# One core: other places for the weight decoding, the pair sums and half of the softmax sums in the first pass of a fused attention and two-layer MLP kernel

## The chip, the core and the metric

The kernel runs on one core of a Trainium2 chip. The engines are TensorE (PE, with its weight loads PEld), VectorE (DVE), ScalarE (ACT), GpSimd (POOL) and SyncE (SP), which issues nearly all DMAs. Each engine works through its own queue in order; an instruction whose inputs or buffer aren't ready holds everything behind it on that engine. The metric is the device time of one launch in microseconds (us), as the median of several runs.

## What is computed

```python
def _attn_ref(q, k, v):                      # 8 batches, 8 heads, 576 tokens, 64 dims
    k_p = k.reshape(B, H, Sp, pool, D).mean(axis=3)      # pooled by 8: 72 keys
    v_p = v.reshape(B, H, Sp, pool, D).mean(axis=3)
    scores = scale * np.matmul(q, k_p.transpose(0, 1, 3, 2))
    attn = softmax(scores)
    return np.matmul(attn, v_p)
x = attention, as 4608 tokens x 512
h = x @ w_in; g = h * np.cos(h); x = g @ w_out                    # 512 -> 2048 -> 512
h = x @ w2_in; solu = h * softmax(h); x = layernorm(solu) * g_ln; out = x @ w2_out   # 512 -> 1024 -> 512
```

The weights come as float64 and are turned into float32 on the core by integer work on their two words. Every product is made of three float32r matmuls of high and low parts.

## The kernel before

The tokens are cut into nine blocks of 512. Pass one makes `h = x @ w_in` for all blocks and stores `g`; pass two multiplies by `w_out`; the last part does the second layer. The change is in pass one.

Pass one is written by hand as a list of places. A block has eight units, a unit eight places: 64 places (`BL`) a block. At each place PE gets three `h` matmuls (`h_mm`, line 652) and then whatever other work was put there with `put(place, function)`; every engine's queue gets its instructions in that order. A place fixes only the order, not a time: an engine runs ahead until something it needs is late. In the numbering here, block 1 starts with the first score matmul at 117.78 us of the trace; block 0 lies before it.

While a block's `h` matmuls run, its places also carry:

- the chain of `h * cos(h)` for the units before: ACT lines 663 and 669, DVE lines 666 and 671;
- the attention of the next token block (`Attn.plan`). Scores of four head pairs at places 0 to 21, their maxima and subtractions on DVE (lines 422, 423) three places behind, exponentials on ACT at 13 and 25. Then, for each half of the heads, `norm`: row sums and reciprocals on DVE (lines 499 to 503, at 16 and 28), and three places later the scaling on POOL (lines 509, 514). Then for each half two transpositions of the scaled weights (`e_tr`, line 550, tile eTp) with one of the left-over part between them (`e_tr_left`, eLp), at 27, 30, 33 and 42, 45, 48, and the products with v (`av`, line 577, tile xo) at 36, 39 and 51, 54. Each of these writes a PSUM tile of the pool `ps_a`, which has two buffers; ACT copies the tile out (eT, eL, x), DVE subtracts that copy from it (lines 555, 533, 580), and only then is the buffer free for the second transposition, score or product behind it;
- the pooling of the next k and v on POOL (lines 231, 259, 273) and the preparation of v (`prep_v`: POOL, ACT and, as its third step, four DVE instructions, lines 367 to 372);
- the weights of the later layers, 24 chunks of 128x512 (`Chunk.plan`). Each is loaded into one of two `raw` buffers, opened by two ACT instructions (`s1`, lines 114 and 115), unpacked by three DVE instructions (`bits`, lines 119, 123, 127) and joined on POOL (`join`, line 139). Chunks 0 to 7 are `w2_in`; each four are followed by `weight_sums` (four DVE subtractions, line 804) and `weight_parts`. Chunks 8 to 23 are `w_out`; each two are followed by `w_sums`, called pair sums here (four DVE instructions, line 877).

Before, a chunk stands every 16 places, at places 0, 16, 32 and 48 of a block; the `w_out` chunks begin 32 places later than that row would have it, so block 3 has chunks at 32 and 48 only, and blocks 4 to 6 at all four.

Of the kernel before, what the change touches and what calls it, by code (L numbers as in the profile page):

```python
# [35 lines left out]
def fused_kernel(ctx, tc, qT_d, kT_d, vN_d, vM_d, vL_d, w_in, w_out, w2_in, w2_out, g_ln, out):  # L36
# [4 lines left out]
    nc = tc.nc  # L41
# [7 lines left out]
    KD = DM // P  # L49
# [51 lines left out]
    class Chunk:  # L101
# [43 lines left out]
        def s3(self):  # L145
            self.done(self)

        def plan(self, put, o, raw, ahead=10):
            put(o - ahead, self.load, raw)
            put(o, self.s1)  # L150
            put(o + 4, self.bits)
            put(o + 7, self.join)
            if self.g is not None:
                put(o + 10, lambda: nc.vector.tensor_scalar(
                    out=self.f, in0=self.f, scalar1=self.g, scalar2=None, op0=ALU.mult))
            self.done(put, o, self)
# [5 lines left out]
    def two(put, o, hi, lo, f):  # L162
        put(o, lambda: nc.scalar.activation(out=hi(), in_=f(), func=AF.Copy))
        put(o + 2, lambda: nc.gpsimd.tensor_tensor(
            out=lo(), in0=f(), in1=hi().bitcast(F32), op=ALU.subtract))
# [214 lines left out]
    class Attn:  # L380
# [206 lines left out]
        def plan(self, put):  # L587
            new = [b for _, _, b, s in self.sg if s == 0 and b > 1]
            nxt = [b for _, _, b, s in at[self.j + 1].sg if s == 0] if self.j < NB - 1 else []

            def staged(pos, make, *a):

                fns = []
                put(pos[0], lambda: (fns.extend(make(*a)), fns[0]()))
                for i, q in enumerate(pos[1:]):
                    put(q, lambda i=i: fns[i + 1]())

            if self.j == 1:
                for i in range(2):
                    put(2 + 4 * i, add, 1, 1, KV[i])  # L600
                    put(17 + 8 * i, pool_vn, 1, i)
                    staged((20 + 8 * i, 22 + 8 * i, 24 + 8 * i), prep_vn, 1, i)
            for p in range(NPAIR):
                for u in range(2):
                    o = 6 * p + 3 * u
                    staged((o, o + 3), self.scores, p, u)
                put((13, 13, 25, 25)[p], self.exp, p)
            for b in new:
                staged((14, 17, 21), prep_v, b)
            for hf in range(2):  # L610
                o = (16, 28)[hf]
                staged((o, o + 3), self.norm, 2 * hf, 2 * hf + 1)
                o = 27 + 15 * hf
                for i, (fn, n) in enumerate((
                        (self.e_tr, 2 * hf), (self.e_tr_left, hf), (self.e_tr, 2 * hf + 1),
                        (self.av, 2 * hf), (self.av, 2 * hf + 1))):
                    d = (2, 4) if fn == self.av else (1, 3)
                    staged((o + 3 * i, o + 3 * i + d[0], o + 3 * i + d[1]), fn, n)
            for p in range(NPAIR):
                if self.j > 1:  # L620
                    put(-10 + 6 * p, self.load_q, p)
            for b in new:
                for i in range(6):
                    put(-10 + 2 * i, kv_load, b, i // 3, KV[2 + i % 3])
                    put(2 * i + i // 3, add, b, i // 3, KV[2 + i % 3])
            for b in nxt:
                for i in range(4):
                    put(32 + 3 * i, kv_load, b, i // 2, KV[i % 2])
                    put(42 + 3 * i, add, b, i // 2, KV[i % 2])

    NQ = NF // 2
# [174 lines left out]
    def weight_parts(put, o, i):  # L806

        k, n = divmod(i, 4)
        t = {}

        def tile():
            if not t:
                t[0] = wo.tile([P, 2, BLK], F32R, "tw")
            return t[0]

        two(put, o, lambda: tile()[:, 0], lambda: tile()[:, 1],
            lambda: whole[((k, 0), (k, 1), (KH + k, 1), (KH + k, 0))[n]])
        put(o + 6, put_away, wd_tw[i], tile)
# [46 lines left out]
    def w_whole(f):  # L865
        w_f[f] = ap1.tile([P, BLK], F32, tag=("qT", "e")[f % 2], name="wf", bufs=2)
        return w_f[f]
# [13 lines left out]
    def w_chunk(f):  # L881
        q = f // 2

        def done(put, o, c):
            if q < 6:
                put(o + 9, lambda: nc.sync.dma_start(out=wf[2 * q][:, 1 - f % 2], in_=w_f[f]))
            if f % 2:
                put(o + 10, w_sums, q)
                if q < 6:
                    put(o + 13, lambda: nc.sync.dma_start(  # L890
                        out=wf[2 * q + 1].rearrange("p a (b n) -> p (a b) n", n=NH), in_=w_s[q]))
                else:
                    w_parts(put, o + 13, q)
        return Chunk(w_out_w[f], done, whole=lambda: w_whole(f))

    wq = {(q, k): dram.tile([P, 2 if k < 3 else 1, 2, NH], F32R, tag=f"wq{k}", name=f"wq{q}{k}", bufs=2)
# [2 lines left out]
    def w_parts(put, o, q):  # L899
        t = {}  # L900

        def part(k, w):
            if k not in t:
                t[k] = wo.tile([P, 2 if k < 3 else 1, 2, NH], F32R, "wp")
            return t[k][:, :, w]

        for i, (k, c, src) in enumerate((
                (0, slice(0, 2), lambda: w_s[q][:, 0:2]), (1, slice(0, 2), lambda: w_s[q][:, 2:4]),
                (2, slice(0, 1), lambda: w_f[2 * q + 1][:, 0:NH]),
                (2, slice(1, 2), lambda: w_f[2 * q][:, 0:NH]),  # L910
                (3, slice(0, 1), lambda: w_f[2 * q][:, NH:BLK]))):
            def end(w, k=k, c=c):
                x = part(k, w)[:, c]
                return x if k < 2 else x.rearrange("p a n -> p (a n)")
            two(put, o + 2 * i, lambda end=end: end(0), lambda end=end: end(1), src)
        for k in range(4):
            put(o + (4, 6, 10, 12)[k], lambda k=k: nc.sync.dma_start(
                out=wq[q, k].bitcast(F32), in_=t[k].bitcast(F32)))
# [244 lines left out]
    def new_raws(tag):  # L1163
        return [xp.tile([P, BLK, 2], I32, tag=tag, name=f"raw{i}") for i in range(4)]
# [26 lines left out]
    with tc.manual_schedule():  # L1191
        raws = new_raws("x0")
# [91 lines left out]
        SL = 2 * KD  # L1284
        BL = NQ * SL
        work = [[] for _ in range(BL * NB + SL * NQ)]

        def put_at(j):
            def put(pos, fn, *a):
                work[BL * (j - 1) + pos].append(lambda: fn(*a))  # L1290
            return put
# [5 lines left out]
        raws = [ap1.tile([P, BLK, 2], I32, tag=t, name="raw") for t in ("em", "eT")]  # L1297
# [3 lines left out]
        chunks += [w_chunk(f) for f in range(NF)]  # L1301
        put = put_at(2)
        for i, c in enumerate(chunks):
            c.plan(put, 2 * SL * (i + 2 * (i // NQ > 0)), raws[i % 2])
        for k in range(KH):
            o = 2 * SL * KD * (k + 1) + 3
            put(o, weight_sums, k)
            for i in range(KD):
                weight_parts(put, o + 4 + 6 * i, KD * k + i)
        put = put_at(NB)  # L1310
        for q, o in enumerate((4, 11, 18, 25, 32, 42)):
            put(o - 9, w_load, q)
# [41 lines left out]
        raws = [wo.tile([P, BLK, 2], I32, "raw", 12 + i) for i in range(2)]  # L1354
# [6 lines left out]
        for m in range(len(units)):  # L1361
            j, q = units[m]
# [100 lines left out]
        a, b, c = NTL - 4, NTL - 3, NTL - 2  # L1463
# [72 lines left out]
```

## Time and profile before

| | |
|---|---|
| median of 3 runs | 1343.4 us (1339.92 to 1344.93) |
| the profiled execution | 1341.87 us |
| its span, first to last instruction | 1340.0 us |
| PE busy | 1305.3 us, 97% |
| DVE busy | 1053.8 us, 79% |
| ACT busy | 697.1 us, 52% |
| POOL busy | 500.7 us, 37% |
| mean granted PE clock | 0.992 of full speed |

Pass one with its attention lies between about 75 and 566 us, pass two and the second layer behind it. A busy PE is a PE with a matmul under way; where it waits, the trace names the instruction that released it.

### The profile page before, as it was taken

To read this page: it belongs to the slowest core of one execution; us is meant where nothing else is said; L and a number is where in the kernel's file an instruction comes from. 1 tells how busy PE (TensorE), PEld (TensorE's weight loads), DVE (VectorE), ACT (ScalarE), POOL (GpSimd) and SP (SyncE) were. 2 spreads that over 40 slices of the span, in tenths; PEclk is the share of its full clock that TensorE was granted. 3 is DMA by queue.
4 is the path that set the end of the run, shared out by engine and by line. 5 is a ranking of instruction groups with operands and counts; after the bars stand their busy time and mean duration, and the time that the engine had idled before them with its cause. 6 is when DMAs were issued, how large, how long until landed. Compare 5 with 4: busy or idle time off the path is not lost. (4 is left out here: it accounts for less than half of the span.)

```text
span 1340.0 us, 20553 instructions
## 1 busy us (share of the span) xinstructions
PE 1305.3 (97%) x7574; PEld 1139.2 (85%) x7574; DVE 1053.8 (79%) x1675; ACT 697.1 (52%) x987; POOL 500.7 (37%) x668
## 2 busy tenths in 40 slices
PE   6889999999999999999999999999999999999998
PEld 5768777887887888899999999999878888888887
DVE  7798887978879785779889899885777767676753
ACT  4576765756566576634444444443544444444432
POOL 3497676765544243501100001101443434343410
PEclk8899999999999999999999999999999999999999
DMA  8425666674655446665555455568411111111101
GB/s 287 169 83 189 217 240 217 235 258 161 236 202 203 149 183 237 221 244 147 156 155 168 141 173 170 153 212 323 146 40 48 40 55 40 56 40 56 40 25 40
DMA packets 82133, 206.09 MB, mean 154 GB/s; under 512 B 7920, under 2 KB 26352, under 8 KB 82032
## 3 DMA queue, kind: packets, MB, share of 16 engines
q1 hardware_dynamic: 81888, 204.77, 44.9%
q8 instruction: 60, 0.98, 0.3%
q14 instruction: 41, 0.34, 0.1%
q10 hardware_dynamic: 144, 0.00, 0.0%
HBM read 125.57 MB, written 79.17 MB: 153 GB/s over the span
## 5 line engine op out<-in xcount | busy, mean ns | idle before, releaser
L652 PE MATMUL h<-x,w 128*128 128x512 f32 x1728 | 434.8, 400 | 0.3 <-DVE t L671 0.3
L652 PEld LDWEIGHTS h<-x,w 128*128 128x128 f32 x1728 | 316.2, 189 | 64.3 <-issue 2.8
L744 PE MATMUL y<-g,wy 128*128 128x256 f32 x3024 | 363.8, 283 | 1.7 <-DVE g L718 1.1
L744 PEld LDWEIGHTS y<-g,wy 128*128 128x128 f32 x3024 | 363.2, 192 | 2.3 <-DVE g L718 1.5
L716 ACT CAST g<-gs 128x1024 fp32r<-128x1024 f32 x72 | 75.7, 1051 | 173.2 <-PE y L744 82.3
L139 POOL TENSOR_TENSOR dec<-dec,raw 128x512 int32<-128x512 int32 x24 | 33.7, 1403 | 240.2 <-DVE dec L127 227.9
L718 DVE TENSOR_TENSOR g<-gs,g 128x1024 fp32r<-128x1024 f32 x72 | 90.3, 1254 | 34.6 <-ACT g L716 32.3
L669 ACT ACTIVATE t<-t,cst 128x1024 f32<-128x1024 f32 x72 | 83.0, 1152 | 57.5 <-DVE t L666 57.4
L671 DVE TENSOR_TENSOR t<-t,h 128x1024 f32<-128x1024 f32 x72 | 87.3, 1213 | 18.0 <-ACT t L669 18.0
L974 POOL TENSOR_TENSOR yl<-yr,yh 128x1024 fp32r<-128x1024 f32 x18 | 44.0, 2446 | 153.8 <-ACT yh L969 153.8
L663 ACT ACTIVATE t<-h 128x1024 int32<-128x1024 f32 x72 | 73.3, 1019 | 42.9 <-PE h L652 42.9
L666 DVE SCALAR_TENSOR_TENSOR t<-t,h 128x1024 f32<-128x1024 int32 x72 | 87.2, 1211 | 1.2 <-ACT t L663 1.2
L231 POOL TENSOR_TENSOR kvraw<-kvraw 128x256 f32<-128x256 f32 (+1 forms) x124 | 80.4, 648 | 12.0 <-DMA kvraw<-in_vL 2.3
L1105 POOL TENSOR_TENSOR sc<-sc,cst 128x1 f32<-128x1 f32 x36 | 20.4, 566 | 140.5 <-DVE sc L1094 113.1
L1140 ACT COPY o<-o 128x512 f32<-128x512 f32 x36 | 21.2, 588 | 96.7 <-PE o L1158 96.7
L698 DVE TENSOR_TENSOR gs<-gr,gs 128x256 f32<-128x256 f32 x136 | 65.9, 484 | 4.7
L718 DVE TENSOR_TENSOR g<-gr,g 128x768 fp32r<-128x768 f32 x68 | 69.1, 1016 | 0.0
L1156 PE MATMUL o<-w,lh 128*128 128x512 f32 x176 | 69.0, 392 | 0.0
L1158 PE MATMUL o<-w,ll 128*128 128x512 f32 x176 | 68.5, 389 | 0.0
L1157 PE MATMUL o<-w,lh 128*128 128x512 f32 x176 | 68.5, 389 | 0.0
L139 POOL TENSOR_TENSOR wf<-dec,raw 128x512 int32<-128x512 int32 x24 | 31.4, 1308 | 67.9 <-DVE dec L127 35.7
L716 ACT CAST g<-gr 128x768 fp32r<-128x768 f32 x68 | 56.6, 832 | 0.0
(191 smaller groups left out, 2571.6 us busy)
## 6 DMA issues: line engine op xcount, KB each, us to landing
gd<-t SPq DMA_DIRECT2D x72, 512.0 KB, 3.0
gr<-gd SPq DMA_DIRECT2D x68, 512.0 KB, 4.0
raw<-in_w_in SPq DMA_DIRECT2D x24, 512.0 KB, 4.8
raw<-in_w_out SPq DMA_DIRECT2D x24, 512.0 KB, 5.1
kvraw<-in_kT SPq DMA_DIRECT2D x32, 288.0 KB, 4.4
qT<-in_qT SPq DMA_DIRECT2D x36, 256.0 KB, 4.7
yd<-yo SPq DMA_DIRECT2D x36, 256.0 KB, 4.6
yr<-yd SPq DMA_DIRECT2D x18, 512.0 KB, 4.2
```

Of the source, the lines that this page charges most:

```text
L231: nc.gpsimd.tensor_tensor(out=x[:, 0:m], in0=x[:, 0:m], in1=x[:, m:2 * m], op=ALU.add)
L652: nc.tensor.matmul(h_ps[n][:, i], lhsT=w[:, a, kk, :], rhs=x[:, b], start=(kk == 0 and m == 0), stop=(kk == KD - 1 and m == 2),)
L663: nc.scalar.activation(out=t.bitcast(I32), in_=h, func=AF.Copy, scale=1.0 / TWO_PI, bias=0.25)
L666: nc.vector.scalar_tensor_tensor(out=t, in0=t.bitcast(I32), scalar=-TWO_PI, in1=h, op0=ALU.mult, op1=ALU.add)
L669: nc.scalar.activation(out=t, in_=t, func=AF.Sin, bias=halfpi)
L671: nc.vector.tensor_tensor(out=t, in0=t, in1=h, op=ALU.mult)
L716: nc.scalar.copy(out=o, in_=f)
L718: nc.vector.tensor_tensor(out=o, in0=f, in1=flat(g[i - 1])[:, 0:n * NH].bitcast(F32), op=ALU.subtract)
L744: nc.tensor.matmul(y_ps[j][i][:, NH * c:NH * (c + 1)], lhsT=w[:, a, P * c:P * (c + 1)], rhs=g[y][b], start=(q == 0 and c == 0 and k == 0), ...
L1156: nc.tensor.matmul(ps, lhsT=hi, rhs=w[:, 0], start=(c == 0), stop=False)
L1157: nc.tensor.matmul(ps, lhsT=hi, rhs=w[:, 1], start=False, stop=False)
L1158: nc.tensor.matmul(ps, lhsT=lo, rhs=w[:, 0], start=False, stop=(c == NF2 - 1))
```

## The change

The chunks of a block stand at places 28, 35, 44 and 51 (28, 37, 50 and 51 for the first eight), four in each of blocks 1 to 6. A chunk is loaded 8 places ahead, not 10, and joined 6 places behind its opening, not 7. The pair sums and what follows them are two places later behind their chunk. `weight_sums` goes from place 3 to 7 of its block, and its parts stand 8 places apart, not 6. In the attention the row sums of the second half of heads go from 28 to 32 (their scaling from 31 to 35), and the third step of `prep_v` from 21 to 25.

```diff
-        def plan(self, put, o, raw, ahead=10):
+        def plan(self, put, o, raw, ahead=8):
             put(o - ahead, self.load, raw)
             put(o, self.s1)
             put(o + 4, self.bits)
-            put(o + 7, self.join)
+            put(o + 6, self.join)
...
-                staged((14, 17, 21), prep_v, b)
+                staged((14, 17, 25), prep_v, b)
             for hf in range(2):
-                o = (16, 28)[hf]
+                o = (16, 32)[hf]
                 staged((o, o + 3), self.norm, 2 * hf, 2 * hf + 1)
...
             if f % 2:
-                put(o + 10, w_sums, q)
+                put(o + 12, w_sums, q)
                 if q < 6:
-                    put(o + 13, lambda: nc.sync.dma_start(
+                    put(o + 15, lambda: nc.sync.dma_start(
                         out=wf[2 * q + 1].rearrange("p a (b n) -> p (a b) n", n=NH), in_=w_s[q]))
                 else:
-                    w_parts(put, o + 13, q)
+                    w_parts(put, o + 15, q)
...
         for i, c in enumerate(chunks):
-            c.plan(put, 2 * SL * (i + 2 * (i // NQ > 0)), raws[i % 2])
+            c.plan(put, BL * (i // 4) + ((28, 37, 50, 51) if i < NQ else (28, 35, 44, 51))[i % 4], raws[i % 2])
         for k in range(KH):
-            o = 2 * SL * KD * (k + 1) + 3
+            o = BL * (k + 1) + 7
             put(o, weight_sums, k)
             for i in range(KD):
-                weight_parts(put, o + 4 + 6 * i, KD * k + i)
+                weight_parts(put, o + 3 + 8 * i, KD * k + i)
```

DVE's queue in block 4 before, from the last score subtraction (place 24) to the subtraction behind the first transposition (eT, place 30) and the one behind the left-over part (eL, place 33); ws are the pair sums, sm the row sums, t the chain:

```order
L423 TENSOR_TENSOR e<-sc,mx 128x288
L877 TENSOR_TENSOR ws<-wf 128x256
L877 TENSOR_TENSOR ws<-ws,wf 128x256
L877 TENSOR_TENSOR ws<-wf 128x256
L877 TENSOR_TENSOR ws<-wf,ws 128x256
L671 TENSOR_TENSOR t<-t,h 128x1024
L666 SCALAR_TENSOR_TENSOR t<-t,h 128x1024
L499 TENSOR_REDUCE sm<-e 128x8 x2
L502 TENSOR_SCALAR sm<-sm 128x16
L503 RECIPROCAL sm<-sm 128x16
L555 TENSOR_TENSOR eT<-eTp,eT 128x512
L533 SCALAR_TENSOR_TENSOR eL<-eLp,cst,eL 128x512
```

The same stretch of DVE's queue now, from behind the third step of `prep_v`; dec is the unpacking of a chunk:

```order
L671 TENSOR_TENSOR t<-t,h 128x1024
L666 SCALAR_TENSOR_TENSOR t<-t,h 128x1024
L555 TENSOR_TENSOR eT<-eTp,eT 128x512
L499 TENSOR_REDUCE sm<-e 128x8 x2
L502 TENSOR_SCALAR sm<-sm 128x16
L503 RECIPROCAL sm<-sm 128x16
L119 TENSOR_SCALAR dec<-dec 128x512
L123 TENSOR_SCALAR dec<-dec 128x512
L127 SCALAR_TENSOR_TENSOR dec<-raw,dec 128x512
L533 SCALAR_TENSOR_TENSOR eL<-eLp,cst,eL 128x512
```

The pair sums and the row sums no longer stand ahead of eT; the row sums and one unpacking stand between eT and eL.

ACT's queue in block 4 before, from the copy behind the first transposition (eT) to that of the left-over part (eL) and of the second transposition; L114 and L115 open a chunk:

```order
L554 CAST eT<-eTp 128x512
L669 ACT_TABLE_LOAD
L669 ACTIVATE t<-t,cst 128x1024
L532 CAST eL<-eLp 128x512
L663 ACTIVATE t<-h 128x1024
L114 ACTIVATE dec<-raw 128x512
L115 ACTIVATE raw<-raw 128x512
L554 CAST eT<-eTp 128x512
```

And now:

```order
L554 CAST eT<-eTp 128x512
L114 ACTIVATE dec<-raw 128x512
L115 ACTIVATE raw<-raw 128x512
L669 ACT_TABLE_LOAD
L669 ACTIVATE t<-t,cst 128x1024
L532 CAST eL<-eLp 128x512
L663 ACTIVATE t<-h 128x1024
L554 CAST eT<-eTp 128x512
```

The opening of a chunk stands ahead of eL's copy now, where it stood behind it. PE's own order is the same in both kernels.

## Rows read from the trace of the kernel before

**Rows 1.** Windows: us, PE, PEld, DVE, ACT, POOL busy, clock, DMA share, GB/s.
```profile
235.77:290.30 54.53, 54.53 (x282) 46.06 (x281) 45.76 (x68) 33.20 (x43) 37.29 (x58) 1.00 0.63 224
290.30:347.95 57.65, 56.43 (x289) 45.78 (x288) 47.10 (x75) 34.93 (x44) 32.15 (x55) 1.00 0.61 212
...
560.00:1340.00 780.00, 773.21 (x4959) 701.68 (x4957) 600.74 (x994) 342.80 (x479) 174.38 (x215) 1.00 0.36 117
```

**Rows 2.** Waits of PE, 98 to 520 us: total us, times, longest.
```profile
PE eTp L550 <- DVE eT L555: 7.2, 5, 1.9
PE sc L414 <- DVE e L423: 0.7, 2, 0.4
PE h L652 <- DVE t L671: 0.3, 1, 0.3
```

**Rows 3.** Timeline of PE in block 4: start, us, work [idle before <- releaser].
```profile
316.76 0.60 PE L528 MATMUL eLp<-ident,el 128*128 128x128 f32 x4
...
320.66 0.66 PE L550 MATMUL eTp<-ident,em 128*128 128x128 f32 x4 [1.22 <-DVE eT L555]
...
323.23 0.60 PE L577 MATMUL xo<-eT,vM 128*128 128x320 f32 x3
```

**Rows 4.** Timeline of PE in block 3, the same two transpositions.
```profile
260.85 0.60 PE L528 MATMUL eLp<-ident,el 128*128 128x128 f32 x4
...
263.38 0.60 PE L550 MATMUL eTp<-ident,em 128*128 128x128 f32 x4
```

**Rows 5.** Timeline of PE in block 2, behind its longest wait.
```profile
206.90 0.66 PE L550 MATMUL eTp<-ident,em 128*128 128x128 f32 x4 [1.92 <-DVE eT L555]
207.32 3.51 PE L652 MATMUL h<-x,w 128*128 128x512 f32 x9
...
212.09 2.23 PE L652 MATMUL h<-x,w 128*128 128x512 f32 x9
```

**Rows 6.** Window of block 2 around that wait.
```profile
206.50:215.00 8.50, 8.10 (x37) 7.01 (x38) 7.14 (x10) 5.64 (x9) 5.60 (x9) 0.80 1.00 322
```

**Rows 7.** Timeline of DVE in block 4, places 20 to 30.
```profile
308.66 1.40 DVE L123 TENSOR_SCALAR dec<-dec 128x512 int32<-128x512 int32 x1
...
314.43 0.42 DVE L877 TENSOR_TENSOR ws<-wf 128x256 f32<-128x256 f32 x1
...
318.16 1.40 DVE L499 TENSOR_REDUCE sm<-e 128x8 f32<-128x576 f32 x2
...
319.97 0.63 DVE L555 TENSOR_TENSOR eT<-eTp,eT 128x512 fp32r<-128x512 f32 x1
```

**Rows 8.** Windows of block 4 before and behind the wait.
```profile
290.30:316.07 25.77, 25.77 (x133) 20.14 (x132) 23.19 (x42) 18.68 (x23) 13.32 (x21) 1.00 0.56 204
320.50:347.95 27.45, 27.29 (x141) 23.18 (x142) 19.55 (x28) 13.02 (x19) 18.52 (x34) 1.00 0.65 220
```

**Rows 9.** Timeline of ACT in block 4.
```profile
315.20 0.57 ACT L554 CAST eT<-eTp 128x512 fp32r<-128x512 f32 x1
...
318.27 1.15 ACT L669 ACTIVATE t<-t,cst 128x1024 f32<-128x1024 f32 x1 [1.21 <-DVE t L666]
319.33 0.57 ACT L532 CAST eL<-eLp 128x512 fp32r<-128x512 f32 x1
```

**Rows 10.** Timeline of POOL in block 4.
```profile
308.30 1.48 POOL L365 TENSOR_TENSOR vM<-vw,vM 128x512 fp32r<-128x512 f32 x1
```

**Rows 11.** Timeline of PE in block 0.
```profile
79.12 0.66 PE L550 MATMUL eTp<-ident,em 128*128 128x128 f32 x4 [2.22 <-DVE eT L555]
```

**Rows 12.** Window of the end of block 0.
```profile
80.00:100.00 20.00, 18.25 (x95) 14.84 (x94) 19.72 (x27) 15.06 (x23) 17.09 (x22) 1.00 0.28 109
```

**Rows 13.** Lines 123, 127 and 109 by source, 98 to 520 us.
```profile
L123 DVE TENSOR_SCALAR dec<-dec x27: 426/429/1404, 101.1 to 482.1; 128x512 int32<-128x512 int32 x27
...
L127 DVE SCALAR_TENSOR_TENSOR dec<-raw,dec x27: 691/693/1659, 102.6 to 482.7; 128x512 int32<-128x512 int32 x27
...
DMA to landing us min/median/max: 4.1/5.3/8.0
```

## The prediction

> **What bounds the kernel now.** I read the windows first. From 560 us on PE is busy 773.2 of 780 us [rows 1]; nothing that the change touches lies there, so no time is won or lost behind pass one. In pass one a block costs 54.5 us where PE never waits (block 3) and 57.65 in block 4, where PE is busy 56.4 of it [rows 1]. So PE bounds pass one too, and what can be won is only what PE waits. The waits name it: from 98 to 520 us, five waits of the transposition eTp for DVE's eT, 7.2 us in all, and 1.0 us of smaller ones [rows 2]. The timeline shows which transposition that is: always the second of the first half, at place 33. In block 4 it starts 3.90 us behind eLp's start (316.76 to 320.66), in block 3 2.53 us (260.85 to 263.38) [rows 3, 4]. It needs the PSUM buffer of the first transposition, which DVE's eT frees.
>
> Why is eT late? ACT's copy before it was done at 315.77 (315.20 + 0.57) [rows 9]; DVE came to eT at 319.97 [rows 7], 4.2 us later, busy all the while: 23.2 of the 25.8 us up to 316.07, and 19.6 of 27.45 behind the wait [rows 8]. DVE has enough time in the block, but its work is bunched ahead of place 30. Block 3 is the control that the trace offers: it has no chunk in its first half, DVE's total is as large (45.8 against 47.1), and it has no wait [rows 1, 4].
>
> **The change part by part.** *First half.* Ahead of eT in DVE's queue there no longer stand, in block 4: the unpackings of the chunks at 0 and 16, at medians and with the first of their three instructions as long as the second 0.43 + 0.43 + 0.69 = 1.55 each, the second of them 1.0 more because its L123 took 1.40 instead of 0.43 [rows 7, 13]; the pair sums, 4 x 0.42 = 1.7 [rows 7]; the row sums, 1.4 and two short ones, 318.16 to 319.97 = 1.8 [rows 7]. That is 1.55 + 2.5 + 1.7 + 1.8 = 7.6 us against a lateness of 4.2. The third step of `prep_v` stays ahead, four places later. So eT follows ACT's copy at once, at about 316.4, and the transposition that wants its buffer at 316.76 + 2.53 = 319.3 finds it free, with 2.9 us to spare. In blocks 2 and 3 `weight_sums` stays in the first half, as block 3 of before had it without a wait.
>
> What that wait costs is more than its idle time: 3.90 - 2.53 = 1.37 against 1.22 named, 0.15 for each restart. Five waits: 7.2 + 0.75 = 8.0 us. In block 2 the wait of 1.92 was followed by nine matmuls in 3.51 us where the next nine took 2.23 [rows 5], in a window with a granted clock of 0.80 [rows 6], a mean of the two levels 2.4 and 1.2 GHz. That is 1.3 us in those nine, and at most 0.2 x 8.5 = 1.7 over the window; I take 1.5. The two score waits (0.7) and the one of h (0.3) stand where unpackings or pair sums filled DVE, at the start and at the end of blocks; I count 1.0. Together 10.5 us.
>
> *Second half.* The block's work is the same, so what left the first half comes here: two more unpackings (3.1 without holds), one more set of pair sums (1.7) and the row sums (1.8, now behind eT): 6.6 on top of 19.6 = 26.2 us [rows 8]. The time for it runs from 316.4 to the block's end, 347.95 less the 1.4 won, 30.1 us. It fits with 3.9 us left. Whether it fits in the order that PE needs is the question, and the first place is the product `av` at place 36: it needs eL, and row sums and an unpacking stand ahead of eL now. Step by step: eT done at 316.4; row sums to 318.2; unpacking to 319.8. ACT copies eL behind the opening of the chunk now, two instructions of some 0.6: but that fills a stretch in which ACT waited 1.21 us for DVE [rows 9], so the copy is done at about 319.9, as before (319.33 + 0.57). DVE's eL, about as long as eT's 0.63, ends at 320.6. PE reaches `av` at 323.23 - 1.37 = 321.9 [rows 3]. 1.3 us to spare; with one L123 of 1.40 on the way 0.3, with a second long instruction nothing. Behind it unpackings stand at 39, 48 and 55 and pair sums at 47, ahead of copies that PE wants some three places later. POOL helps here: its join waits for the unpacking ahead of it in its own queue, so POOL mostly stands still while DVE unpacks. I bound what comes back at 0 and 1 us per block and take 0.25, nearer to the ledger's 3.9 us left: 6 x 0.25 = 1.5.
>
> *What I cost at nothing.* The scaling on POOL four places later: row sums are done at 318.2 instead of 319.97, so POOL gets its input sooner. PE wants the result only at place 42. Stores and pair sums two places later: nothing reads them in pass one. Block 0: its transposition waits 2.22 us [rows 11], and its row sums move behind eT and eL. But DVE is full there, 19.7 of 20 us [rows 12], with the same work to do before the block's last copies, so what is won at the first transposition is waited for at the last; between 0 and 1 us, I take 0. The loads, 8 places ahead: a place is 54.5 / 64 = 0.85 us on average [rows 1], so 6.8 us against a landing of 4.1 to 8.0, median 5.3 [rows 13]; SP issues them as soon as the store before them is off, ahead of PE's place, so I count none late.
>
> Sum: 1341.87 - 10.5 + 1.5 = 1332.9 for an execution like the profiled one. The median of the runs is 1.5 above that execution, which would give 1334.4. I forecast the middle, 1333.5.
>
> **The rivals.** *The second half gets crowded by holds.* L123 took 0.43 at its median and 1.40 in block 4, where it started at 308.66 while POOL's vM ran from 308.30 to 309.78; L127 reached 1.66 against 0.69 [rows 7, 10, 13]. One hold is about 1 us. The second half is where POOL is busy (18.5 of 27.45 us, against 13.3 of 25.8 in the first) [rows 8], and four unpackings stand there now instead of two. With one or two holds each, 4 to 8 us meet 3.9 us left, and the products at 36 and 54 wait. At 1 us a block six waits give back 6: 1341.9 - 10.5 + 6 = 1337.4, with the median's offset 1338. Against it: POOL's join waits for the very unpacking. The Trainium skill ("SBUF — State Buffer", section "Who interferes with whom") says that a DVE instruction with two SBUF inputs, or one that uses both port pairs, and a POOL instruction shut each other out for the whole length of the one that began first; the case in block 4 agrees with it. By that rule alone moving unpackings under POOL's work is the wrong way, and this rival is what it would do. Chance 0.17.
>
> *The wait only moves.* DVE has row sums and unpacking between eT and eL, and if `av` at 36 waits for eL as long as the transposition did, 1.4 us a block, nothing changes: 1342 to 1343. For it: the margin of 1.3 us rests on one block's times, and the openings of chunks are new ahead of ACT's eL copy. Against it: DVE starts the stretch 3.5 us earlier than before (316.4 instead of 319.97). Chance 0.09.
>
> *Slower: the raw loads come late.* ACT's opening at 28 would wait for a load, and behind it in ACT's queue stand eL's copy and the sine. The load has 6.8 us instead of 8.5 (ten places), and the loads at 36 and 43 wait for POOL's join two places earlier. At the longest landing seen, 8.0, the opening is 1.2 late and `av` just holds. It costs from there on, and decides the sign where `av` waits more than 9 / 6 = 1.5 us a block, a landing of about 9.5 us. At 11 us, 3.0 a block and a lower clock behind each as in block 2 (1.3), the sum is 1341.9 - 10.5 + 6 x 4.3 = 1357. Against it: no landing that long was seen. Chance 0.09.
>
> **How the numbers follow.** 0.5% of the median, 6.7 us, is about what a measurement tells from no change. My forecast, with 0 to 0.6 us a block coming back, runs from 1329 to 1336.7 and has 0.65: all of it faster. The crowded half (1336.7 to 1341) and the moved wait are within 0.5%: 0.26. Slower: 0.09. The range reaches to 1341 and leaves out the slow rival, most of the moved wait and some 0.03 below 1329.
>
> **What the profile would show.** Right: no wait of eTp for eT from 98 to 520 us; DVE's eT within 0.5 us of ACT's copy; blocks 1 to 6 within 2 us of each other but for their attention shapes; a clock of 1.00 in block 2; DVE busier behind place 30 than ahead of it. The crowded half: waits of xo for eL or eT, L123 and L127 near 1.4 in blocks 1 to 6. The moved wait: one wait of xo per block for eL. The loads: ACT's L114 idle for a DMA. I am wrong in the main if PE waits in pass one sum to more than 5 us, or if they go and the time does not follow.

## The result, and the profile after

| | before | after |
|---|---|---|
| median of 6 runs each, same session | 1343.07 us (1339.92 to 1344.93) | 1329.23 us (1328.46 to 1331.27) |
| ratio | | 0.9903 [0.9888, 0.9919] |
| the profiled execution, its span | 1341.87, 1340.0 us | 1331.27, 1329.5 us |
| PE busy | 1305.3 us, 97% | 1302.5 us, 98% |
| DVE busy | 1053.8 us, 79% | 1053.0 us, 79% |

The changed kernel is faster: by 13.8 us in these medians, by 10.6 between the two profiled executions. (A later session gave 8.3 us; the experiments say where that scatter is.) The engines do the same work as before; what went is waiting.

The waits of PE from 60 to 570 us of the changed kernel (total us, times, longest), to be read against [rows 2]:

```profile
PE eTp L550 <- DVE eT L555: 1.3, 1, 1.3
PE xo L577 <- DVE eL L533: 1.0, 1, 1.0
PE eLp L528 <- DVE x L580: 0.8, 1, 0.8
PE y L744 <- DVE t L671: 0.6, 1, 0.6
...
```

All but the one of y (at 556 us, as long before) lie in block 0. From 100 to 556 us PE waits for nothing, where [rows 2] had 8.2 us. So each block is as long as its matmuls; these are blocks 1 to 6, whose attention shapes alternate (columns as in [rows 1]):

```profile
119.50:174.81 55.31, 55.31 (x282) 46.90 (x280) 44.31 (x66) 36.84 (x49) 37.13 (x57) 1.00 0.61 211
174.81:231.03 56.22, 56.22 (x290) 46.50 (x288) 48.39 (x71) 39.15 (x53) 44.54 (x60) 1.00 0.68 243
231.03:285.54 54.51, 54.51 (x282) 46.16 (x281) 51.57 (x77) 37.80 (x50) 42.53 (x60) 1.00 0.78 279
285.54:341.72 56.18, 56.18 (x290) 45.96 (x289) 47.34 (x75) 35.18 (x45) 34.12 (x55) 1.00 0.65 224
341.72:396.97 55.25, 55.25 (x282) 46.94 (x280) 47.09 (x75) 35.09 (x45) 32.85 (x52) 1.00 0.66 221
396.97:454.14 57.17, 57.17 (x289) 47.16 (x288) 47.19 (x77) 37.17 (x50) 24.82 (x35) 1.00 0.51 174
...
549.50:1329.50 780.00, 773.31 (x4959) 701.66 (x4957) 601.03 (x994) 342.94 (x479) 173.55 (x215) 1.00 0.36 117
```

Before, the six blocks took 57.12, 60.87, 54.53, 57.65, 57.62 and 58.29 us. Block 3, the control that had no wait, is the one that gained nothing (54.53 to 54.51). The last 780 us hold the same PE work to 0.1 us, as [rows 1] had it.

Block 4, place by place. PE's two transpositions and the first product behind them, against [rows 3]:

```profile
312.01 0.60 PE L528 MATMUL eLp<-ident,el 128*128 128x128 f32 x4
...
314.53 0.60 PE L550 MATMUL eTp<-ident,em 128*128 128x128 f32 x4
...
317.03 0.60 PE L577 MATMUL xo<-eT,vM 128*128 128x320 f32 x3
```

The second transposition now follows eLp by 2.52 us without a wait, as block 3 of before had it [rows 4]. What DVE did meanwhile, against [rows 7]:

```profile
311.05 0.69 DVE L555 TENSOR_TENSOR eT<-eTp,eT 128x512 fp32r<-128x512 f32 x1 [0.77 <-ACT eT L554]
311.66 1.40 DVE L499 TENSOR_REDUCE sm<-e 128x8 f32<-128x576 f32 x2
...
313.47 0.36 DVE L119 TENSOR_SCALAR dec<-dec 128x512 f32<-128x512 f32 x1
313.87 0.43 DVE L123 TENSOR_SCALAR dec<-dec 128x512 int32<-128x512 int32 x1
314.33 0.69 DVE L127 SCALAR_TENSOR_TENSOR dec<-raw,dec 128x512 int32<-128x512 int32 x1
315.12 0.75 DVE L533 SCALAR_TENSOR_TENSOR eL<-eLp,cst,eL 128x512 fp32r<-128x512 f32 x1
```

and ACT, against [rows 9]:

```profile
310.45 0.57 ACT L554 CAST eT<-eTp 128x512 fp32r<-128x512 f32 x1
310.91 0.67 ACT L114 ACTIVATE dec<-raw 128x512 f32<-128x512 f32 x1
...
314.52 0.56 ACT L532 CAST eL<-eLp 128x512 fp32r<-128x512 f32 x1
```

eT starts 0.03 us behind the end of ACT's copy (310.45 + 0.57), where it started 4.2 behind it; now DVE waits for ACT, 0.77 us. Row sums, unpacking and eL follow in the order that the prediction stepped through. eL is done at 315.87 and PE reaches the product at 317.03: 1.2 us to spare, as in blocks 1, 5 and 6; in blocks 2 and 3 it is 0.6. The two halves of the block, against [rows 8]:

```profile
285.54:311.46 25.92, 25.92 (x133) 20.29 (x132) 20.52 (x35) 15.28 (x18) 12.37 (x22) 1.00 0.54 196
...
314.53:341.72 27.19, 27.19 (x143) 23.21 (x142) 23.89 (x34) 16.86 (x25) 21.74 (x33) 1.00 0.76 255
```

DVE went from 23.2 and 19.6 us to 20.5 and 23.9: the same work (47.1 and 47.3 us in the whole block), spread to where the time was.

### The profile page after: what moved, and what is told of

Its sections match the earlier page's. It is cut to its first block, busy times and chain, and to the rows that moved or that the text cites. A ratio compares the mean times of both kernels' runs of the same rounds, so it can differ in the third digit from the quotient of the medians.

```text
span 1329.5 us, 20583 instructions
## 1 busy us (share of the span) xinstructions
PE 1302.5 (98%) x7574; PEld 1140.3 (86%) x7574; DVE 1053.0 (79%) x1675; ACT 697.9 (52%) x987; POOL 504.5 (38%) x668
```

## The experiments

Two questions stood after the result. First, which of the change's numbers removes the wait: by theory A a wait is only what lateness exceeds the room, so any part that takes off enough removes it, and the parts replace each other; by theory B each part brings its own share and the shares add up. Second, why medians say 13.8 us and profiles 10.6: scatter of the run's start (C), or the low clock in block 2 (D). From each profile, one per kernel and session, I took the start of block 1 (the first score matmul behind 98 us) and what is left of the span behind it (us):

| | span | block 1 starts | from there on |
|---|---|---|---|
| before | 1340.0 | 117.78 | 1222.2 |
| before, again | 1340.4 | 120.34 | 1220.1 |
| after | 1329.5 | 119.50 | 1210.0 |
| after, again | 1330.1 | 119.71 | 1210.4 |
| row sums alone | 1330.7 | 116.46 | 1214.2 |
| chunks alone | 1331.1 | 120.53 | 1210.6 |
| two more DVE instructions | 1333.1 | 117.81 | 1215.3 |
| four more DVE instructions | 1350.0 | 118.29 | 1231.7 |
| loads at 4 | 1326.5 | 116.25 | 1210.3 |
| a step at the start moved | 1323.1 | 113.66 | 1209.4 |

**Row sums alone.** The kernel before with one number changed:

```diff
-                o = (16, 28)[hf]
+                o = (16, 32)[hf]
```

> The kernel before with one number of the change: the row sums of the second half of heads at place 32, everything else where it was. Theory A (DVE's bunching ahead of eT is what PE waits for, and PE's wait is only the part of eT's lateness that passes the 2.9 us of room behind eLp): taking the row sums, 1.8 us, from ahead of eT is as much as the waits were (0.9 to 1.9 us), so the five waits of the transposition fall from 7.2 to under 1 us in all, and with restarts and block 2's clock the time falls by 8 to 10 us, nearly the whole gain. Theory B (the chunks in the first half are what matters): the row sums move 1.8 of 7.6 us, the gain is a quarter, 2 to 3 us, or nothing because eL, behind the row sums now, makes the product at place 36 wait 1 us or more in each block.

1332.11 us against 1340.74, ratio 0.9929 [0.9914, 0.9944]. Waits of PE from 100 to 520 us:

```profile
PE h L652 <- DVE t L671: 1.1, 2, 0.7
PE sc L414 <- DVE e L423: 0.8, 2, 0.5
PE xo L577 <- DVE eL L533: 0.4, 1, 0.4
```

The listed waits for eT are gone with 1.8 us less ahead of it, and DVE in its block 4 shows how:

```profile
312.46 0.68 DVE L555 TENSOR_TENSOR eT<-eTp,eT 128x512 fp32r<-128x512 f32 x1
```

eT ends at 313.14; PE's transposition starts at 313.58, without a wait. In block 2, which had the longest wait, there is nothing to spare: eT ends at 202.10 and the transposition follows at once, 2.77 us behind eLp's start where 2.52 is the undisturbed distance:

```profile
202.16 0.66 PE L550 MATMUL eTp<-ident,em 128*128 128x128 f32 x4
```

In blocks 1 and 5, too, it starts 0.06 us behind eT's end. One number brings most of the gain. It leaves 2.3 us of small waits, and from block 1 on this kernel is 3.9 us behind the whole change (1214.2 to about 1210.3), 1.9 of it in block 2, 1.0 in block 4 and 0.75 in block 5.

**Chunks alone.** The changed kernel with row sums and `prep_v` back at their old places:

```diff
-                staged((14, 17, 25), prep_v, b)
+                staged((14, 17, 21), prep_v, b)
...
-                o = (16, 32)[hf]
+                o = (16, 28)[hf]
```

> The changed kernel with the attention's two numbers put back: row sums at place 28 and the third step of prep_v at 21. The chunks, pair sums and weight_sums stand at their new places. Theory A: 5.8 us of unpackings and pair sums leave the space ahead of eT against waits of 0.9 to 1.9 us, so the waits of eTp go as well and the gain is 9 to 11 us, all of it again: the two parts replace each other. Theory B: the gain is the whole less what the row sums bring, 7 to 11 us. A and B differ in the sum of this run's gain and that of the row sums alone: about twice the whole by A, about the whole by B.

1331.41 us (1329.09 to 1338.38), ratio 0.9932 [0.9909, 0.9956]; PE has no wait from 100 to 520 us, and from block 1 on it takes 1210.6 us, as the whole change does. In block 0 the first transposition waits 2.22 us (at 81.75), as it did in [rows 11].

The two parts bring 8.6 and 9.3 us by their medians on one chip; by B both together would bring 18, and they brought 8.3 to 13.8 in two other sessions. The profiles say the same without the scatter of the start: from block 1 on, against the two profiles of before, the row sums bring 5.9 to 8.0 us, the chunks 9.5 to 11.6, and the whole change 9.7 to 12.2. A holds, B falls.

Moving the chunks does all that the change does behind block 0; moving the row sums besides it buys room. With the chunks alone eT starts 0.8 to 2.1 us behind the end of ACT's copy in blocks 1 to 6, with the whole change 0.03 or 0.04; in block 3 the product follows eL's end at once (0.06 us) and the block is 0.3 us longer, where the whole change has 0.6 us to spare. The row sums at 32 also keep POOL away from the first unpacking of a block. At 28 they release POOL's scaling (313.37 to 315.51 in block 4) just when DVE unpacks, and that unpacking takes 2.2 or 2.3 us in each of the six blocks; with the whole change it takes 1.48 in each.

**More work in every unpacking.** The changed kernel with two, then four, further DVE instructions of line 119's form in each of the 24 unpackings, 0.9 and 1.8 us a chunk; they repeat a clamp and change no value:

```diff
-        def bits(self):
+        def bits(self, extra=0):
...
+            for _ in range(extra):
+                nc.vector.tensor_scalar(
+                    out=t.bitcast(F32), in0=t.bitcast(F32), scalar1=WORD_MIN, scalar2=WORD_MAX,
+                    op0=ALU.max, op1=ALU.min,
+                )
...
-            put(o + 4, self.bits)
+            put(o + 4, self.bits, 2 if self.g is None else 0)
```

(4 in place of 2 in the second kernel; lines from 119 on stand five higher in both.)

> The changed kernel with two more instructions of the form of L119 (0.42 us, a clamp that changes nothing the second time) ahead of each of the 24 unpackings: 0.9 us more DVE work per chunk, 3.6 a block. If the room in the second half is what the changed kernel's trace shows (eL done 1.2 us before the product at place 36 starts, the last eT 2.5 us before the product at 54), PE still doesn't wait, and the time is that of the changed kernel, 0 to 2 us more. If the second half is full, so that DVE's work there sets PE's pace, it is 24 x 0.9 = 21 us more.

1333.54 us, ratio 0.9944 [0.9926, 0.9961]; waits of PE from 100 to 520 us:

```profile
PE eTp L555 <- DVE x L585: 1.7, 1, 1.7
PE eLp L533 <- DVE x L585: 0.3, 1, 0.3
...
```

> The same with four more: 1.8 us more per chunk. By the room of 1.2 and 2.5 us: the product at 36 waits some 0.6 us in each of six blocks, and the one at 54, behind three chunks and 5.4 us of extra work, some 2; with restarts and now and then a lower clock 12 to 20 us more than the changed kernel. If the room is larger than the trace lets one read: under 4 us more. If the second half were full already: 24 x 1.8 = 43 us more.

1350.42 us, ratio 1.0069 [1.005, 1.0087]; the same query:

```profile
PE eTp L555 <- DVE x L585: 5.6, 4, 2.6
PE xo L582 <- DVE eL L538: 3.7, 6, 1.1
PE h L657 <- DVE t L676: 3.0, 2, 1.8
PE xo L582 <- DVE eT L560: 2.4, 3, 0.9
PE eLp L533 <- DVE x L585: 1.8, 2, 1.5
...
```

Two more instructions a chunk cost 5 us from block 1 on, where I had expected up to 2; four cost 22, where I had expected 12 to 20. By the medians it is 1.6 to 4.3 and 18.5 to 21.2 us above the changed kernel's two medians, which come from other sessions. The added instructions were busy for 26.8 and 51.3 us in the profiles, somewhat more than the 21 and 43 worked out. The first miss has a place: with two more all listed waits lie in blocks 2 and 3, which carry the weight parts as well (DVE 48.4 and 51.6 us above) and had 0.6 us to spare at the product, not 1.2. These two blocks are 1.2 and 3.0 us longer than in the changed kernel, block 4 is 0.4 longer, blocks 1, 5 and 6 at most 0.1. So the work is nearly free in blocks 4 to 6, where I had the room from, and not in blocks 2 and 3. With four more the wait for eL at the product stands in all six blocks, 0.40 us long in block 4, where the changed kernel had 1.2 to spare.

**Both kernels again, on another chip.** No edit.

> The kernel before once more, unchanged. In the two profiled executions the change takes 10.6 us, all of it named waits, restarts and one stretch at a lower clock; the medians differ by 13.8. Theory C (scatter of the start): both kernels run at a lower clock somewhere from 20 to 60 us and leave it sooner or later by 2 us, whatever the change; then a fresh profile of before shows the same stalls of 8 us, a block 0 that starts within 2 us of the other, and lowest times of before and after that differ by 10 to 11. Theory D (stalls cost clock in more executions than the one profiled): a fresh profile shows a clock below 1.00 behind other stalls of blocks 1 to 6 too, or none in block 2, and the spread of before's times (5.8 us) stays about twice that of the changed kernel.

> The changed kernel once more, unchanged, on the same chip. No wait of PE from 100 to 560 us and a clock of 1.00 there in any execution; its times differ only by where the clock rises between 20 and 60 us: 1327 to 1332. By theory C its lowest time is 10 to 11 below before's lowest, by theory D the medians differ by 12 or more while the lowest times differ by less.

Before: 1341.05 against 1340.18, ratio 1.0005 [0.9996, 1.0015]. After: 1331.91, ratio 0.9931 [0.9918, 0.9944]. So the gain is 8.3 us here and was 13.8 in the first session; the lowest times of all runs on this chip are 1338.95 and 1328.36, 10.6 apart. In the second profile of before the waits repeat (eTp for eT: 7.2 us, five times, 1.9 the longest, from 100 to 520 us) and the clock in block 2 doesn't. This window holds its longest wait (1.91 us, at 209.50); the granted clock in it is 1.00:

```profile
206.00:218.00 12.00, 10.09 (x53) 8.43 (x53) 11.15 (x17) 9.67 (x13) 8.58 (x11) 1.00 0.91 318
```

In the first profile the same window has 0.86:

```profile
206.00:218.00 12.00, 11.10 (x53) 9.54 (x54) 9.61 (x14) 7.16 (x11) 8.35 (x14) 0.86 0.89 303
```

So each theory is half right. D: the low clock is not in every execution. Where it was, it cost 1.6 us: block 2 took 60.87 us in the first profile and 59.29 in the second, with the same wait. But the medians differ by 8.3 us here, where D wanted 12 or more, and the spreads of 6.8 and 4.3 us are not two to one. C: the lowest times differ by 10.6, as it said. What scatters is the start, by more than the 2 us that it allowed: block 1 starts at 117.78 and 120.34 in before, at 119.50 and 119.71 in after, and from 116.25 to 120.53 over all kernels whose work ahead of block 0 is not edited. In the windows of 20 to 60 us the clock differs from execution to execution; the kernel before in its second profile:

```profile
20.00:60.00 40.00, 31.85 (x146) 25.35 (x147) 28.51 (x49) 19.28 (x40) 16.99 (x16) 0.72 0.61 216
```

In its first, which started block 1 2.6 us earlier, it was 0.79. The clock there doesn't account for the start alone: 0.79 stands beside starts of 117.78 and 119.71, 0.87 beside 116.25 and 118.29.

**Loads four places ahead.** The changed kernel with half the lead, to test the rival of late loads:

```diff
-        def plan(self, put, o, raw, ahead=8):
+        def plan(self, put, o, raw, ahead=4):
```

> The changed kernel with the chunks loaded 4 places ahead of their opening, not 8. A load then has 4 x 0.85 = 3.4 us by PE's place, against a landing of 3.9 to 5.7 in the changed kernel's trace. If SP issues a load as soon as the store ahead of it in its queue is off, some 3 to 7 places early, the openings wait 0 to 1 us and PE not at all: 0 to 2 us more than the changed kernel. If loads are issued at PE's place (the slow rival of the prediction), each opening is 0.5 to 2.3 us late, eL's copy behind it too, and PE waits up to 1 us a block: 3 to 8 us more, with L114 idle for the DMA.

1328.39 us, ratio 0.9909 [0.9893, 0.9924]. ACT's opening (line 114) does wait for loads now; what ended its idle time from 98 to 520 us (us, times):

```profile
  DMA raw<-in_w_in: 2.1, 1
  DMA raw<-in_w_out: 1.5, 2
```

PE waits for nothing from 100 to 550 us, and from block 1 on it takes 1210.3 us. Even a lead of four places, 3.4 us, harms nothing. That its profiled execution is shorter than that of the changed kernel (1326.5 against 1330.1 us) comes from the start (block 1 at 116.25, with a clock of 0.87 from 20 to 60 us against 0.79), which the edit doesn't touch; for the medians that is likely and not shown.

**A step of the start moved.** In the changed kernel the longest wait of PE that is left stands ahead of the attention's first blocks:

```profile
48.80 1.30 PE L414 MATMUL sc<-kT,qT 128*128 128x144 f32 x4 [4.10 <-DVE e L423]
```

DVE unpacks the first weights there, and its instructions are long, ahead of e (48.19 to 48.65):

```profile
44.70 1.42 DVE L123 TENSOR_SCALAR dec<-dec 128x512 int32<-128x512 int32 x1
46.15 1.63 DVE L127 SCALAR_TENSOR_TENSOR dec<-raw,dec 128x512 int32<-128x512 int32 x1
```

These unpackings are taken from a queue, `pipe`, one step at some places of each unit. The edit leaves out the first step and takes one more at the end:

```diff
-                if s == 1 and pipe.busy or s == 5 and n < Q0 - 1:
+                if s == 1 and n > 0 and pipe.busy or s == 5 and n < Q0:
                     pipe.step()
```

> A further version: the changed kernel with the first step of w_in's chunks in pass one's unit 0 left out and one added at the end of that row (unit 4), so that in block 0 every unpacking of w_in from place 1 on stands four places later. PE waits 4.1 us at 48.8 us of the changed kernel's trace for a score subtraction that stands on DVE behind two unpackings, held up by POOL to 3.4 us each, and runs at a lower clock behind it. If that is the cause, the wait falls to under 1.5 us and the time by 3 to 6 us. If the unpackings are wanted by h as early as they stand, the wait moves to h, 0 to 2 us less. The waits of block 0 from 80 to 98 us (3.6 us) may grow by 1 to 2, since that work comes later.

1324.9 us (1324.33 to 1330.96), ratio 0.9895 [0.9877, 0.9913]; 7.0 below the changed kernel's median on the same chip (1331.91), more than the 3 to 6 expected, and the intervals of the two ratios don't overlap, though by little. The wait shrinks:

```profile
45.52 0.73 PE L414 MATMUL sc<-kT,qT 128*128 128x144 f32 x4 [0.63 <-DVE e L423]
```

and the start is denser: PE is busy for 35.3 us of the 40 from 20 to 60 us (30.8 in the changed kernel), at a clock of 0.87. The waits of block 0 grow from 3.6 to 4.9 us, as expected. Block 1 starts at 113.66, the earliest of all. The wait is 3.5 us shorter; whether the other 3.5 us belong to the edit is not shown. The kernel with loads at 4, on the same chip, has the unedited start, the same wait as the changed kernel (4.12 us) and a clock of 0.87 too: against it the median is 3.5 us lower, with overlapping intervals, and block 1 starts 2.6 us earlier. By its median it is the fastest kernel that was run.

## Why the prediction was right, and where it was off

**The wait and its cause: right.** The prediction named DVE's eT, late by work bunched ahead of it, and the waits of eTp for eT from 98 to 520 us went from 7.2 us to none. eT starts 0.03 or 0.04 us behind the end of ACT's copy in all six blocks. Block 3 gained nothing, the others did. The step through eT, row sums, unpacking and eL came out in block 4 with a margin of 1.2 us where 1.3 had been worked out; blocks 2 and 3, which were not stepped through, have 0.6.

**More was moved than needed.** 7.6 us taken from a lateness of 4.2 was enough, but the count that decides is another: eT has the 2.9 us of room that the prediction worked out, so of the 4.2 us only 1.3 was a wait (1.22 in the trace). Row sums alone, 1.8 us, removed it, with 0.4 to spare in block 4 and nothing in blocks 1, 2 and 5.

**What comes back, 1.5 us: it was 0.** This is the term that was mis-sized, and it stood in for the rival of holds. The second half does hold four unpackings, and the work there is what the prediction counted: DVE is busy for 26.6 us from the end of eT to the end of block 4, where 26.2 of 30.1 had been worked out:

```profile
311.65:341.72 30.07, 30.07 (x158) 25.53 (x157) 26.64 (x41) 19.71 (x27) 21.74 (x33) 1.00 0.75 250
```

Yet PE waits nowhere, and not because the holds stayed away. L123 and L127 by source, from 98 to 520 us of the changed kernel, against [rows 13]:

```profile
L123 DVE TENSOR_SCALAR dec<-dec x27: 427/446/1401, 102.9 to 446.2; 128x512 int32<-128x512 int32 x27
...
L127 DVE SCALAR_TENSOR_TENSOR dec<-raw,dec x27: 691/707/1677, 104.3 to 446.7; 128x512 int32<-128x512 int32 x27
```

The medians rose by 0.02 us, but they hide the long ones. Of the 24 chunks, 12 now take 2.0 us or more to unpack, up to 2.8, where an undisturbed one takes 1.5; before, 6 did. POOL is at work at the start of every instruction that takes clearly longer than its undisturbed time. In block 2, beside POOL's line 164 (209.87 to 211.35):

```profile
209.07 0.59 DVE L119 TENSOR_SCALAR dec<-dec 128x512 f32<-128x512 f32 x1
...
210.23 1.68 DVE L127 SCALAR_TENSOR_TENSOR dec<-raw,dec 128x512 int32<-128x512 int32 x1
```

In busy time, over all unpackings of that stretch, lines 119, 123 and 127 went from 15.10, 15.70 and 21.84 us to 16.08, 15.29 and 23.36: 2.1 us more in all. The 24 chunks take 46.3 us, some 10 above undisturbed ones, under 2 a block, where the rival had 4 to 8. Where a hold would have counted first, ahead of eL, none came: the first unpacking of a block takes 1.48 us in all six. There the reason that the prediction gave against the rival is what the trace shows: the join waits in POOL's queue for the unpacking, with the scaling behind it, so POOL is idle while DVE unpacks. In block 4 it has been idle for 10.28 us when the join starts, 0.14 us behind the end of L127 (314.33 + 0.69); the trace names ACT's eL copy, which ended 0.06 us later than L127, as its releaser:

```profile
315.16 1.31 POOL L139 TENSOR_TENSOR wf<-dec,raw 128x512 int32<-128x512 int32 x1 [10.28 <-ACT eL L532]
```

For the other three unpackings of a block that reason mostly fails, and their holds fit into the room: the added instructions of the experiment, over 1 us a chunk, were nearly free in blocks 4 to 6 as well. With the chunks alone the first unpacking is held too, and only block 3 is longer for it, by 0.3 us. The long unpackings of the start (1.42 and 1.63 us from 44.70 on, with POOL's join from 44.56 to 45.84 and its split from 45.79 to 47.23 beside them) are the same thing where there is no room.

**The clock in block 2, 1.5 us: 1.6 in that profile, and not always.** The second profile of before had the wait without the low clock: block 2 took 59.29 us, where the first had 60.87, and the nine matmuls behind the wait took 2.33 us, where [rows 5] had 3.51:

```profile
209.50 0.66 PE L550 MATMUL eTp<-ident,em 128*128 128x128 f32 x4 [1.91 <-DVE eT L555]
209.91 2.33 PE L652 MATMUL h<-x,w 128*128 128x512 f32 x9
```

So this part of the gain belongs to some executions only.

**Block 0 at 0: right.** It took 49.89 us from its score on and takes 49.84. The wait of 2.22 [rows 11] is gone, and the one at the last transposition has grown, as the prediction said, with DVE full; before:

```profile
92.14 0.66 PE L550 MATMUL eTp<-ident,em 128*128 128x128 f32 x4 [0.27 <-DVE eT L555]
```

and after:

```profile
93.50 0.66 PE L550 MATMUL eTp<-ident,em 128*128 128x128 f32 x4 [1.30 <-DVE eT L555]
```

**The sum.** 10.5 us without what was to come back, and the spans differ by 10.5. That they agree so well is luck: from block 1 on the gain is 12.2 us, and block 1 started 1.7 us later in the profile of after. Of the 12.2, named waits are 8.2 and the clock 1.6. Another 1.8 is the restart term, which was 0.75 in the prediction: in the second profile of before, at a clock of 1.00, the blocks with waits have that much more busy PE than after (0.64 in block 2, 0.49 in block 5, 0.2 each in blocks 1, 4 and 6); why it is more than 0.15 for each wait is open. The rest, 0.6, lies behind block 6 in the main and is no larger than what two profiles of one kernel differ by there. The chunks of before reach that far: the last two, which the section on the kernel before leaves out, stand at places 0 and 16 of block 7. Against the second profile of before, without the low clock, the gain is 10.1. The median I forecast, 1333.5, is 4.3 above the first session's and 1.6 above the second's; 1.5 of it is the term above, the rest the start and the middle that I took between one execution and the median of three. The first session's median, 1329.23, lies only 0.2 us inside the lower end of the 1329 to 1336.7 that I had forecast.

**The rivals.** Crowded by holds: holds came, smaller than feared, and reached no matmul (above). The wait only moves: no wait of xo for eL in blocks 1 to 6; two more instructions a chunk bring one of 0.2 us into block 3, four bring one into every block. Late loads: at half the lead ACT's 3.6 us of waiting reached no matmul. In the changed kernel one opening waited 0.4 us for its load, and landing took 3.9 to 5.7 us, below the 8.0 of before:

```profile
DMA to landing us min/median/max: 3.9/4.3/5.7
```

## What to carry to other kernels

Read a wait as lateness less room: find the instruction that is late, its own input, and the moment at which its consumer comes; then only the excess has to be moved, and what moves has to meet the next due moment behind it, stepped through in the queue's order. Step through the fullest block too, not only through a typical one. Adding known work until waits appear measures the room that a schedule has left, and shows in which blocks it has none. A median over all instructions of a line can stay while half of them get longer: look at the longest ones, and at what ran beside them. Compare executions from a fixed instruction on when the start scatters by more than the effect.

## What the hardware showed unexpectedly

The same wait of 1.9 us in block 2 was followed by a granted clock below full in one execution of the kernel before (0.86 from 206 to 218 us) and by 1.00 in the other. And the time to block 1 varied from 116.25 to 120.53 us over kernels with the same work ahead of block 0, with a clock of 0.72 to 0.87 in the stretch from 20 to 60 us: that spread of 4.3 us ahead of block 1 compares with 2.1 us behind it for the two profiles of before and 0.4 for those of after.
